# Maxima in a bank of the scores, block sums two at a time, and new instruction lists for one attention-and-FFN kernel

## The chip, the cores and the metric

The kernel runs on one core of a Trainium2 chip, as one program. The metric is the device time of one execution in microseconds, and runs of a kernel are compared by it.

## What is computed

Memory attention for 8 batches of 8 heads, 576 positions and head width 64, with 32 memories a head, and a bilinear feed-forward block behind it, in fp32.

```python
a = np.exp(phi - np.max(phi, axis=2, keepdims=True))
a = a / (np.sum(a, axis=2, keepdims=True) + 1e-09)
k_m = np.einsum('bhsm,bhsd->bhmd', a, k)
v_m = np.einsum('bhsm,bhsd->bhmd', a, v)
scores = scale * np.matmul(q, k_m.transpose(0, 1, 3, 2))
attn = softmax(scores)              # with 1e-09 added to the sum
x = np.matmul(attn, v_m)            # 4608 tokens x 512
out = ((x @ w1) * (x @ w2) @ w3) @ w_out
```

## The kernel before

One batch is 576 tokens, cut into two halves of 288 columns (`HALF`). The weights are prepared in a first phase: 64-bit words are converted to fp32 in five steps a task (C1 to C5), and w3 and w_out are multiplied once (W..., line 611), since no nonlinearity stands between them. After that each batch b does two things at once. Its attention step for batch b+1 or b+2 runs: maxima of phi over the positions (`top`), their exponentials and sums (`exp`, `norm`), the maxima spread over partitions by two transposes (`bm`, line 232, into a PSUM bank of its own), subtracted from a second copy of phi (`bs`, L238 and L242), exponentials (`be`), memories (`mem`, L254 and L263, scaled by `memc`), two transposes of them (`block`, L285, copied out by `blockc` on ScalarE), scores (`sc0`, `sc1`, L303), and the softmax (`scc` transposes into SBUF, `mx`, `sb`, `ex`, `sm`, `mu`, `tr`). M0 to M3 (L420) multiply the value memories with w1 and w2. Meanwhile the products of batch b run: block products P1 to P7 for four quarters q (`block_product`, L748, six matmuls a step and a Strassen-like scheme of seven products for four blocks), then the output units O1 to O7 in two parts (`out_unit`, L833, twelve matmuls a step). All of them are fp32 split into a high and a low part, three matmuls for one.

Between the P and the O steps stand sums of blocks: `first_sum` (tokens f, L789) and `sums` (Sa, Sb, Sc, L800 to L804), each for one block of four, on VectorE or GpSimd. `block_result` (tokens e, L773) adds a kept result in SBUF to one in PSUM, and `block_g` (tokens v, L732) multiplies two results; `a_copy` (tokens c) copies one of the factors.

The order of every engine's instructions is written out by hand in four lists of tokens: FIRST for batch 0 with the weights' phase, SECOND for batch 1, BATCH for batches 2 to 6, LAST for batch 7. Each engine takes its instructions in the order in which the lists name them. A token with a digit names the step, quarter or part; "!" moves a step that can run on two engines to the other one (f, Sa, Sb, Sc run on GpSimd without it and on VectorE with it; l, v and others the reverse). Attention tokens are for batch b+1, with "+" for b+2 and with "-" for b. Loads (`phi2`, `tok2`, `kv2`, `q2`) are issued by SyncE, whose queue also holds the stores of the results (C11 to C22).

PSUM has eight banks, four slots on each of two sides. `Pair` takes the first free slot of each side, and `done` returns them. The order of returns in the list decides which slot the next step takes, and that step waits for the last reader of the slot.

## Time and profile before

| | us |
|---|---|
| median of 3 runs | 497.23 (496.66 to 497.57) |
| the profiled execution | 496.72 |
| its span, from the first to the last instruction | 494.9 |
| TensorE busy | 489.1 |
| VectorE busy | 429.8 |
| ScalarE busy | 339.0 |
| GpSimd busy | 265.2 |

The span lies within the execution's time; the 1.8 us around it are start and end. Busy times are those of instructions, and overlapping instructions of one engine count once. In timelines a line gives the start and duration of one instruction or of several alike that follow each other; since matmuls overlap, the pace of TensorE is read from start to start. "Idle before" stands in square brackets with the engine that ended it.

### The profile page before, as it was taken

To read this page: it belongs to the slowest core of one execution; us is meant where nothing else is said; L and a number is where in the kernel's file an instruction comes from. 1 tells how busy PE (TensorE), PEld (TensorE's weight loads), DVE (VectorE), ACT (ScalarE), POOL (GpSimd) and SP (SyncE) were. 2 spreads that over 40 slices of the span, in tenths; PEclk is the share of its full clock that TensorE was granted. 3 is DMA by queue.
4 is the path that set the end of the run, shared out by engine and by line. 5 is a ranking of instruction groups with operands and counts; after the bars stand their busy time and mean duration, and the time that the engine had idled before them with its cause. 6 is when DMAs were issued, how large, how long until landed. Compare 5 with 4: busy or idle time off the path is not lost.

```text
span 494.9 us, 11317 instructions
## 1 busy us (share of the span) xinstructions
PE 489.1 (99%) x4328; PEld 422.2 (85%) x4328; DVE 429.8 (87%) x812; ACT 339.0 (68%) x718; POOL 265.2 (54%) x256
## 2 busy tenths in 40 slices
...
PEclk9999999999999999999999999999999999999999
...
GB/s 295 411 410 426 426 161 87 248 3 38 255 262 215 3 143 327 11 3 42 318 120 3 24 254 203 3 24 145 311 1 26 81 88 2 25 48 25 2 1 97
DMA packets 22390, 68.89 MB, mean 139 GB/s; under 512 B 1728, under 2 KB 9920, under 8 KB 20288
## 3 DMA queue, kind: packets, MB, share of 16 engines
...
q8 instruction: 34, 0.56, 0.5%
...
## 4 chain that ended last, share of the span: by engine, by line
PE 97%; DMA 1%; ACT 0%; DVE 0%; SPq 0%; issue 0%; DVEq 0%
PE ps L833 36%; PE ps L748 32%; PE ps L611 11%; PE ps L420 6%; PE ps L718 5%; PE ps L254 3%; PE ps L303 2%; DMA raw<-in_w3T 1%; PE ps L263 1%; PE ps L285 0%; PE ps L232 0%; SPq L527 0%; DVE wo L599 0%; ACT w L584 0%; DVE w L599 0%
## 5 line engine op out<-in xcount | busy, mean ns | idle before, releaser
L833 PE MATMUL ps<-sh,Wh 128*128 128x288 f32 x448 | 132.8, 296 | 0.0
L833 PE MATMUL ps<-sh,Wl 128*128 128x288 f32 x448 | 132.2, 295 | 0.0
L833 PE MATMUL ps<-sl,Wh 128*128 128x288 f32 x448 | 132.0, 295 | 0.0
L818 POOL TENSOR_TENSOR sl<-g,sh 128x576 fp32r<-128x576 f32 x43 | 65.3, 1520 | 72.8 <-ACT sh L501 48.9
L833 PEld LDWEIGHTS ps<-sh,Wh 128*128 128x128 f32 x448 | 84.2, 188 | 6.8 <-ACT mh L431 5.0
L833 PEld LDWEIGHTS ps<-sh,Wl 128*128 128x128 f32 x448 | 84.2, 188 | 0.0
L833 PEld LDWEIGHTS ps<-sl,Wh 128*128 128x128 f32 x448 | 84.2, 188 | 0.0
L501 ACT CAST sh<-g 128x576 fp32r<-128x576 f32 x78 | 52.3, 685 | 24.3 <-PE ps L833 14.5
L611 PE MATMUL ps<-wo,w 128*128 128x512 f32 x128 | 55.9, 594 | 0.2 <-DVE w L599 0.2
L767 ACT COPY c<-ps 128x288 f32<-128x288 f32 x112 | 41.6, 411 | 18.9 <-PE ps L748 16.2
L773 DVE TENSOR_TENSOR c<-ps,c 128x288 f32<-128x288 f32 x112 | 44.8, 451 | 10.4 <-ACT c L767 8.4
L748 PE MATMUL ps<-sh,ms 128*128 128x288 f32 x224 | 51.8, 296 | 0.0
L611 PEld LDWEIGHTS ps<-wo,w 128*128 128x128 f32 x128 | 24.0, 190 | 30.4 <-issue 28.3
L728 ACT COPY a_sb<-ps 128x288 f32<-128x288 f32 x72 | 29.0, 406 | 22.7 <-PE ps L748 19.8
L818 DVE TENSOR_TENSOR sl<-g,sh 128x576 fp32r<-128x576 f32 x55 | 43.2, 794 | 0.7 <-ACT sh L501 0.4
L438 DVE TENSOR_TENSOR ml<-ps,mh 128x512 fp32r<-128x512 f32 x64 | 41.0, 682 | 1.3 <-ACT mh L431 1.2
L748 PEld LDWEIGHTS ps<-sh,ms 128*128 128x128 f32 x224 | 38.2, 188 | 1.0 <-ACT ps L761 0.8
L732 DVE TENSOR_TENSOR g<-ps,a_sb 128x288 f32<-128x288 f32 x72 | 32.1, 449 | 6.2 <-ACT a_sb L728 5.0
L456 DVE TENSOR_TENSOR tmp<-ps,tmp 128x256 f32<-128x256 f32 x84 | 32.8, 418 | 4.4 <-ACT mh L431 2.1
L431 ACT CAST mh<-ps 128x512 fp32r<-128x512 f32 x64 | 34.5, 597 | 2.2 <-PE ps L420 1.2
L748 PE MATMUL ps<-ah,mh 128*128 128x288 f32 x112 | 34.6, 309 | 0.0
L748 PE MATMUL ps<-sh,mh 128*128 128x288 f32 x112 | 33.1, 296 | 0.0
...
## 6 DMA issues: line engine op xcount, KB each, us to landing
...
ph<-in_phiT SPq DMA_DIRECT2D x8, 576.0 KB, 4.6
a<-in_phi_tok SPq DMA_DIRECT2D x8, 576.0 KB, 5.7
...
```

Of the source, the lines that this page charges most:

```text
L420: nc.tensor.matmul(ps[t][g * M : (g + 1) * M], lhsT=vm[b % 2][d, g], rhs=w12_sb[q][d, :, g], start=True, stop=True,)
L431: nc.scalar.copy(out=mh[:, t], in_=ms["ps", q][t].rearrange("p (w f) -> p w f", w=2))
L438: nc.vector.tensor_tensor(out=ml[:, t], in0=x, in1=ms[q][0][:, t].bitcast(F32), op=ALU.subtract)
L456: nc.vector.tensor_tensor(out=tmp[:, j], in0=x, in1=tmp[:, y], op=op)
L501: nc.scalar.copy(out=out, in_=in_)
L611: nc.tensor.matmul(pw[r, i // 2][i % 2][:, cols], lhsT=x[:, i * P : (i + 1) * P], rhs=wos[k // half][:, k % half, cols], start=k == 0 and ...
L732: engine.tensor_tensor(out=G[n, f // half][:, f % half], in0=b, in1=a, op=ALU.mult)
L748: nc.tensor.matmul(G[bank, q][w][:, :HALF], lhsT=xs[x][:, w], rhs=ys[y], start=i in (1, 5) and k == 0, stop=i in (2, 3, 4) and k == 2, ski ...
L767: nc.scalar.copy(out=G["kept", i, q][:, j], in_=x)
L773: nc.vector.tensor_tensor(out=c, in0=x, in1=c, op=ALU.add)
L818: flexible().tensor_tensor(out=lo, in0=src, in1=hi.bitcast(F32), op=ALU.subtract)
L833: nc.tensor.matmul(ps[j][:, :HALF], lhsT=piece(x, s, 2 * part + k)[:, jc], rhs=y[:, k], start=i in first and part == 0 and k == 0 and t == ...
```

## The change

- `scores(1)` of batches 2 to 6 calls `spread_max` of the next batch with its own pair of banks: the two transposes go to columns 288 to 415 of the two banks, ahead of the score matmuls. `Pair` counts its users, and both banks are returned when the scores are copied out and the maxima are subtracted. `sub_max` then does its wide addition in two parts, one for each bank. Batches 0 to 2 keep the bank of their own.
- M3 of batches 2 to 6 is followed at once by `block` of the next batch.
- `first_sum` and `sums` take two blocks (`pair_of`) in one instruction.
- `block_result` for product 2 writes its second half back to PSUM, and `block_g` reads it there, always on VectorE; the bank is returned after that.
- The additions of 1e-9 move from VectorE to ScalarE; the reciprocal of `soft_sum` becomes a step of its own, `si`.
- `block_product` looks up the sums of the M blocks only where it uses them.
- All four lists are new.

```diff
 FIRST = """
...
-C4 C3 tok0 kv0 q0 C2 C3 C2 C5 C4 C5 -top -exp W06 -norm C1 C1 C2 C3 C2 C3 W07 -bm C4 C5 K2 Kh2 C4 C5 W101 C1 K3 Kt3
-W100 K1 W111 -bs K0 C4 Kt0 Kl2 C3 Kh1 Kh0 W110 C2 r3 C4 -be -mem C5 C3 Kt2 r0 C1 -memc -block C5 -blockc -sc0 -sc1
--scc0 -scc1 Kt1 W121 W120 -mx0 C3 C2 -sb0 W130 -mx1 -ex0 C2 Kl0 -sb1 C3 W131 W141 C4 -sm0 W140 -ex1 C1 C5 C1 W150 W160
...
-Sc0! O20 Mu0 M1 h21 l21 Sc2 h61 M2 l61 ex0 O21 sm0 O61 ex1 sm1 Sb1! Sb2! h70 l70! h71 mu1 Mr1 mu0 h50 l71 l50! u2 Ms1
...
+W01 W02 C5 C3 C2 C4 C5 W03 W04 W05 -top C1 -exp C1 C2 C3 W06 W07 C4 K1 K2 Kt2 Kt1 C5 C2 K0 K3 -bm Kh1! C4 C3 W100 C1
+-bs W101 C3 W110 Kh0! W111 -be Kh3 C4 C5 -mem C5 Kt3 Kh2 C2 C4 C3 W120 -norm -memc -block -blockc Kl3 C1 C5 -sc0 -sc1
+W130 Kl1 -scc0 -scc1 C3 C2 -mx0 W121 -sb0 -ex0 -mx1 C4 Kl0 -sb1 C2 C3 r1! -ex1 Kl2 Kt0 C1 C5 W131 W141 W140 r0! r3! C1
...
+l11 sb0 A30 a30 l41 sb1 O40 Sa0! Sa1! y0 Sb1 ex0 O11 g30 ex1 O41 Mr0 Ms0 h60 l60 p1 h20 O60 M1 Mt0 l20! sm0 O20 h21
+sm1 Sb0! Mu0 h61 l61 O61 h70 l70 h71 u2 l21 p4 si0 O21 h50 Sc1! q2 Sc0! O70 si1 Mr1 C11 h30 l71 mu1 h51 O71 mu0 Ms1
+Mt1 h31 Mh1 l50! M2 tr0 ah0 tr1 Mu1 l30 Mh2 l51! O50 O51 ah1 al1! p5 O30 l31 al0 T1 T3! Ml1 C21 C22 T2! T4! O31 C12
...
 """
 BATCH = """
-phi2 P10 -M3 s00 s01 P20 c10 v10 P60 k200 k201 P50 P70 k502 P30 e402 v40! e202 -Mr3 -Ms3 v20! P11 P40 s10 s11 c30 v30
-h10! -Mh3 P61 k210 k211 P51 +top -Ml3 -Mt3! P21 k512 P31 c11 e212 +exp -Mu3! P71 +bm P12 e412 P41 f0 v11 s20 s21 c31
-P62 sc1 tok2 +bs l10! v31 sc0 v41 kv2 scc0 scc1 k220 h11! P22 P52 v21! c12 v12 mx2 P13 k522 k221 P32 e222 f3 P72 s30
-+be P53 s31 P23 k532 P63 c13 e422 v42 k230 k231 v22 f1 l11! sb2 P33 e232 f2 P73 e432 v13 P42 Sa0 ex2 Sa1! P43 +mem v43
-c32 v32 Sb0 h20 +norm sm2 +memc M0 Mr0 M2 Sa3 c33 v33 v23! M1 O10 Mh0 Ms0 Ml0 Sb3 O11 Sb1 h21 l21 h50 Sa2! l20! p1 l50
-Sb2! h60 l60 O20 O21 Mh1 Sc1! h61 O60 C11 l61 O61 h51 h70 Mt0 Sc0! mu2 Mh2 u2 tr2 ah0 ah1 Sc2! l51! O50 Sc3! l70 h30
-h71 l71! O51 p5 Mu0 O70 al0 l30 O30 Ml1 h40 l40 T1 h31 l31 Mr1 Ms1 O71 O31 h41! C22 O40 C12 +block q2 l41! Mt1 +blockc
-T3! O41 Mu1 al1 T2 Th1 C21 Tl1 T4! Th0! Mr2 Tl0! Ms2 Mt2! Mu2! Ml2
+P10 s00 s01 -M3 P60 blockc P20 c10 v10 k200 k201 P50 phi2 P70 k502 e402 v40! P30 e202 v20 P11 P40 s10 s11 P61 +top
+-Mr3 c30 v30 k210 k211 -Ms3 -Mt3! P51 k512 P71 e412 -Mh3 h10! -Ml3 P21 P31 e212 v21 P41 P12 +exp f0 c11 v11 sc1 sc0
+c31 v31 v41! s20 s21 l10! scc0 P62 k220 k221 P52 h11 scc1 P72 P22 tok2 +bs k522 e422 f1 P32 -Mu3! c12 l11! v12 P13 s30
+e222 v22 s31 P42 c32 v42! +be P23 mx2 P63 k230 sb2 k231 P53 k532 ex2 kv2 c13 P73 e432 v32 P33 +norm e232 v23 Sa0 P43
+c33 +mem v33 M0 +memc Sb0 v13 Mh0 M2 Mr0 sm2 M1 Mh1 v43! O10 Ms0 Mt0 h21 h20! Ml0 Mu0 si2 O11 p1 l21 h50 Mr1 h60 l20!
+O20 O21 C11 l50 Sc0 Sa1 Sb1! l60 mu2 O50 h51 l51 h61 l61 h70 O60 O61 Mh2 Ms1 tr2 h71 Ml1 u2 h30 l70! O51 h40 l30 l71!
+l40 O70 p5 Sc1! ah0 Mt1 h41 q2 Ml2 O30 O71 al0! C22 O40 l41! O41 Mu1 T1 T3 h31 l31 ah1 al1 T2 T4! O31 Mr2 C12 C21 Ms2
+Th1 Tl1! Th0 Tl0! Mt2! Mu2!
 """
...
@@ -145,7 +144,7 @@
 
 
         def __init__(self, n=2, full=True, seeded=False):
-            self.slots, self.banks = [], []
+            self.slots, self.banks, self.users = [], [], 1
             for side in range(n):
                 slot = next(i for i in free_banks[side] if not seeded or (side, i) in written)
                 free_banks[side].remove(slot)
@@ -160,7 +159,9 @@
             return [(i, self.banks[i][:, :HALF]) for i in range(w.start, w.stop)]
 
         def done(self, *sides):
-            for i in sides or range(len(self.banks)):
+            if not sides:
+                self.users -= 1
+            for i in sides or range(len(self.banks) if self.users == 0 else 0):
                 free_banks[i].append(self.slots[i])
 
     loaded = {}
@@ -202,7 +203,7 @@
             LOADS[what](b)
 
 
-    ready = {}
+    ready, maxima = {}, {}
 
     def attention(b):
 
@@ -220,27 +221,37 @@
                 nc.scalar.activation(
                     out=ph[:, t], in_=ph[:, t], func=AF.Exp, bias=mx[:, t : t + 1], accum_out=sm[:, t : t + 1]
                 )
+            nc.scalar.activation(out=sm, in_=sm, func=AF.Copy, bias=1e-9)
 
         def norm():
-            nc.vector.tensor_scalar_add(v["sm"], v["sm"], 1e-9)
             nc.vector.reciprocal(out=v["sm"], in_=v["sm"])
 
-        def spread_max():
-            v["mxb"] = Pair(1, full=False)
-            ps = v["mxb"][0][:, : NT * P]
+        def spread_max(beside=None):
+            v["bank"] = beside or Pair(1, full=False)
+            if beside:
+                beside.users += 1
+                v["mxb"] = [beside[t][:, HALF : HALF + P] for t in range(NT)]
+            else:
+                v["mxb"] = [v["bank"][0][:, t * P : (t + 1) * P] for t in range(NT)]
             for t in range(NT):
-                nc.tensor.transpose(ps[:, t * P : (t + 1) * P], v["mx"][:, t : t + 1].broadcast_to([P, P]), ident)
+                nc.tensor.transpose(v["mxb"][t], v["mx"][:, t : t + 1].broadcast_to([P, P]), ident)
 
         def sub_max():
-            ps, n = v["mxb"][0][:, : NT * P], NT * P
+            n = NT * P
             v["a"] = loaded.pop(("a", b))
             a = v["a"][:, : 4 * n].rearrange("p (c x) -> p c x", c=4)
-            nc.vector.tensor_tensor(out=a, in0=a, in1=ps.unsqueeze(1).broadcast_to([P, 4, n]), op=ALU.add)
+            if len(v["bank"].banks) == 1:
+                ps = v["bank"][0][:, :n].unsqueeze(1).broadcast_to([P, 4, n])
+                nc.vector.tensor_tensor(out=a, in0=a, in1=ps, op=ALU.add)
             for t in range(NT):
+                if len(v["bank"].banks) == 2:
+                    x = a[:, :, t * P : (t + 1) * P]
+                    ps = v["mxb"][t].unsqueeze(1).broadcast_to([P, 4, P])
+                    nc.vector.tensor_tensor(out=x, in0=x, in1=ps, op=ALU.add)
                 half = slice(t * D, (t + 1) * D)
                 x = v["a"][half, 4 * n :]
-                nc.vector.tensor_tensor(out=x, in0=x, in1=ps[half, t * P : (t + 1) * P], op=ALU.add)
-            v["mxb"].done()
+                nc.vector.tensor_tensor(out=x, in0=x, in1=v["mxb"][t][half], op=ALU.add)
+            v["bank"].done()
 
         def exp_tok():
             nc.scalar.activation(out=v["a"], in_=v["a"], func=AF.Exp)
@@ -297,6 +308,8 @@
             if "q" not in v:
                 v["q"] = loaded.pop(("q", b))
             banks = v["scores", n] = Pair()
+            if n == 1 and 2 <= b < B - 1:
+                maxima[b + 1](banks)
             ps = [banks[t][:, :HALF] for t in range(NT)]
             for g in range(NG):
                 for t in range(NT):
@@ -316,7 +329,7 @@
             for t in range(NT):
                 x = ps[t][:, :HALF].rearrange("p (k m) -> p k m", m=M)
                 nc.vector.transpose(out=v["s"][:, n, t * nb : (t + 1) * nb], in_=x)
-                ps.done(t)
+            ps.done()
 
         def both(n):
             return slice(0, 2) if n == 2 else slice(n, n + 1)
@@ -342,8 +355,10 @@
         def soft_sum(n):
             ss = v["ss", n] = stats(n)
             nc.vector.tensor_reduce(out=ss, in_=v["s"][:, both(n)], axis=AX.X, op=ALU.add)
-            nc.vector.tensor_scalar_add(ss, ss, 1e-9)
-            nc.vector.reciprocal(out=ss, in_=ss)
+            nc.scalar.activation(out=ss, in_=ss, func=AF.Copy, bias=1e-9)
+
+        def soft_inverse(n):
+            nc.vector.reciprocal(out=v["ss", n], in_=v["ss", n])
 
         def soft_mul(n):
             sv, ss = v["s"][:, both(n)], v["ss", n]
@@ -395,9 +410,10 @@
             flexible().tensor_tensor(out=lo, in0=src, in1=hi.bitcast(F32), op=ALU.subtract)
             ready["T", b][n].append(lo)
 
+        maxima[b] = spread_max
         steps = {"top": top, "exp": exp, "norm": norm, "bs": sub_max, "be": exp_tok, "memc": normal, "blockc": spread,
                  "bm": spread_max, "mem": memories, "block": blocks}
-        parts = {"sc": scores, "scc": tokens_down, "mx": soft_max, "sb": soft_sub, "ex": soft_exp, "sm": soft_sum,
+        parts = {"sc": scores, "scc": tokens_down, "mx": soft_max, "sb": soft_sub, "ex": soft_exp, "sm": soft_sum, "si": soft_inverse,
                  "mu": soft_mul, "tr": probs, "ah": probs_high, "al": probs_low, "Th": sums_high, "Tl": sums_low}
         for name, f in parts.items():
             steps |= {f"{name}{n}": lambda f=f, n=n: f(n) for n in range(3)}
@@ -732,9 +748,9 @@
         engine.tensor_tensor(out=G[n, f // half][:, f % half], in0=b, in1=a, op=ALU.mult)
 
     def block_product(b, i, q, G):
-        (mh, ml), (sh, sl) = ready["M", b][q], ready["M", b]["sums", q]
+        of = ready["M", b]
         t, u = {1: (0, 0), 2: (1, 0), 4: (1, 1), 7: (0, 1), 5: (None, 0), 6: (None, 1), 3: (None, 2)}[i]
-        xs = [m[:, t, :, u * P : (u + 1) * P] for m in (mh, ml)] if t is not None else [m[:, u] for m in (sh, sl)]
+        xs = [m[:, t, :, u * P : (u + 1) * P] for m in of[q]] if t is not None else [m[:, u] for m in of["sums", q]]
         if i < 4:
             ys = ready["A", b][{1: (0, 0), 2: (0, 1), 3: (1, 1)}[i]]
         else:
@@ -770,8 +786,8 @@
         bank, kept = {2: ("gamma", 2), 4: ("alpha", 5)}[i]
         for j, x in G[bank, q].parts(w):
             c = G["kept", kept, q][:, j]
-            nc.vector.tensor_tensor(out=c, in0=x, in1=c, op=ALU.add)
-            if i == 2:
+            nc.vector.tensor_tensor(out=x if (i, j) == (2, 1) else c, in0=x, in1=c, op=ALU.add)
+            if (i, j) == (2, 0):
                 G[bank, q].done(j)
 
     def block_g(i, q, G, engine):
@@ -782,15 +798,23 @@
             bank.done(1)
         else:
             c = G["kept", {2: 2, 4: 5}[i], q]
-            g_product(G, n, f, c[:, 0], c[:, 1], engine)
-
-    def first_sum(k, G):
+            if i == 2:
+                g_product(G, n, f, c[:, 0], G["gamma", q][1][:, :HALF], nc.vector)
+                G["gamma", q].done(1)
+            else:
+                g_product(G, n, f, c[:, 0], c[:, 1], engine)
+
+    def pair_of(part):
+        return slice(2 * part, 2 * part + 2)
+
+    def first_sum(part, G):
+        k = pair_of(part)
         low, top = G[1, 0][:, k], G[0, 0][:, k]
         flexible().tensor_tensor(out=low, in0=top, in1=low, op=ALU.subtract)
 
-    def sums(which, k, G):
-
-        gp = flexible().tensor_tensor
+    def sums(which, part, G):
+
+        gp, k = flexible().tensor_tensor, pair_of(part)
         a, s3, a22, a12 = G[0, 0][:, k], G[1, 0][:, k], G[1, 1][:, k], G[0, 1][:, k]
         if "S2" not in G:
             G["S2"] = att.tile([P, NG, S], F32, name="q", tag="q").rearrange("p g s -> p (g s)")[:, : half * HALF]
@@ -906,6 +930,8 @@
                 if name in steps[0]:
                     if at < B:
                         steps[at][name]()
+                    if what == "-M3" and 2 <= b < B - 1:
+                        steps[b + 1]["block"]()
                 elif what in at_stage:
                     next(at_stage[what])()
                     left -= what == "C5"
```

## Rows read from the trace of the kernel before

**Rows 1.** The page, parts 1 and 2: TensorE's busy time, granted clock by slice.

```profile
PE 489.1 (99%) x4328; PEld 422.2 (85%) x4328; DVE 429.8 (87%) x812; ACT 339.0 (68%) x718; POOL 265.2 (54%) x256
...
PEclk9999999999999999999999999999999999999999
```

**Rows 2.** Windows: us; busy PE, PEld, DVE, ACT, POOL; steady, last batch.

```profile
344.86:397.42 52.56, 52.56 (x524) 48.40 (x516) 47.30 (x92) 35.03 (x82) 31.79 (x31) 1.00 0.32 121
452.95:494.90 41.95, 38.67 (x296) 38.23 (x288) 25.88 (x51) 20.54 (x48) 16.86 (x15) 0.99 0.09 29
```

**Rows 3.** TensorE's timeline, steady batch: start us, duration us, engine, line, tiles.

```profile
344.86 0.40 PE L748 MATMUL ps<-ah,mh 128*128 128x288 f32 x1
...
354.50 0.38 PE L232 MATMUL ps<-ident,mx 128*128 128x128 f32 x2
354.64 0.38 PE L748 MATMUL ps<-ah,mh 128*128 128x288 f32 x1
...
358.40 0.40 PE L748 MATMUL ps<-ah,mh 128*128 128x288 f32 x1
```

**Rows 4.** TensorE's timeline, the same stretch one batch later.

```profile
397.42 0.40 PE L748 MATMUL ps<-ah,mh 128*128 128x288 f32 x1
...
410.65 0.40 PE L748 MATMUL ps<-ah,mh 128*128 128x288 f32 x1
```

**Rows 5.** TensorE's timeline, end of a batch and M3 of the next.

```profile
341.15 0.38 PE L285 MATMUL ps<-ident,kvm 128*128 128x128 f32 x2
341.29 0.38 PE L833 MATMUL ps<-sh,Wh 128*128 128x288 f32 x1
...
343.84 1.09 PE L420 MATMUL ps<-w,vm 64*32 64x512 f32 x16
```

**Rows 6.** TensorE's timeline, transposes between matmuls of the first phase.

```profile
37.06 0.38 PE L232 MATMUL ps<-ident,mx 128*128 128x128 f32 x2
37.28 1.02 PE L611 MATMUL ps<-wo,w 128*128 128x512 f32 x2
```

**Rows 7.** TensorE's timeline, first phase: block transposes, M0 and M1, first products.

```profile
47.10 0.59 PE L285 MATMUL ps<-ident,kvm 128*128 128x128 f32 x2 [0.53 <-ACT kvm L276]
...
67.00 1.95 PE L420 MATMUL ps<-w,vm 64*32 64x512 f32 x32
68.88 3.70 PE L611 MATMUL ps<-wo,w 128*128 128x512 f32 x8
...
72.69 0.29 PE L718 MATMUL ps<-ah,ml 128*128 128x288 f32 x1
```

**Rows 8.** VectorE's timeline, first phase: `Ml0`.

```profile
68.81 1.28 DVE L438 TENSOR_TENSOR ml<-ps,mh 128x512 fp32r<-128x512 f32 x2
```

**Rows 9.** VectorE's timeline, the steady batch of rows 3: Ms3, v30, `+top`.

```profile
349.52 1.20 DVE L456 TENSOR_TENSOR tmp<-ps,tmp 128x256 f32<-128x256 f32 x3
350.79 0.46 DVE L732 TENSOR_TENSOR g<-ps,a_sb 128x288 f32<-128x288 f32 x1
351.16 1.34 DVE L214 TENSOR_REDUCE mx<-ph 128x2 f32<-128x1152 f32 x1
```

**Rows 10.** SyncE's timeline there, and DMA issues: size, median us to landing.

```profile
344.17 0.46 SPq L170 DMA_DIRECT2D ph<-in_phiT  x1
...
ph<-in_phiT SPq DMA_DIRECT2D x8, 576.0 KB, 4.6
```

**Rows 11.** Groups by line and shape: count, busy us, mean ns, idle before.

```profile
L818 POOL TENSOR_TENSOR sl<-g,sh 128x576 fp32r<-128x576 f32 x43 | 65.3, 1520 | 72.8 <-ACT sh L501 48.9 <-issue 17.7 <-DVE g L804 5.1
...
L773 DVE TENSOR_TENSOR c<-ps,c 128x288 f32<-128x288 f32 x112 | 44.8, 451 | 10.4 <-ACT c L767 8.4 <-ACT a_sb L728 1.0 <-PE ps L748 0.9
L818 DVE TENSOR_TENSOR sl<-g,sh 128x576 fp32r<-128x576 f32 x55 | 43.2, 794 | 0.7 <-ACT sh L501 0.4
...
L345 DVE TENSOR_SCALAR st<-st 128x36 f32<-128x36 f32 x6 | 4.7, 778 | 0.2
...
L232 PE MATMUL ps<-ident,mx 128*128 128x128 f32 x16 | 3.1, 275 | 0.0
```

More of the change, by code (lines that the diff above doesn't have):

```diff
@@ new lines @@
+-tr0 C5 -M1 -tr1 s0 s1 C4 -ah0! -al0 C5 -Mh1 Q1! -ah1! C3 -Ml0 W171 Dt2 A01 -Ml1 Dt0 -al1! C4 Dt3 F3 a01 A00 C1 C2 g01
+C5 a00 F0 g00 A11 -M2 D2 E2 Et2 a11 D3 C1 g11 E3 -Mh2 Et3 Et0 phi1 -Ml2 C3 C1 Q2! A03 C4 C4 A10 a03 g03 A23 C5 C3 F2
+a23 g23 A12 a10 r2 w2! A02 D1 a12 g10 A13 top s2 C5 a02 g02 t0 exp y2 bm z0 a13 Dt1 F1 g12 tok1 bs A22 g13 h10 a22 A20
+Et1 w3 t2 be kv1 -M3 -Mh3 E1 a20 mem D0 f0 q1 -Ml3 norm A33 h11 memc block w1 Q0 blockc g22 f1 A32 y3 t3! g20 z3 E0
+h40 y1 a32 Q3 sc1 l10! w0 g32 a33 sc0 scc0 mx0 g33 t1 z1 M0 Mh0 Ml0 l40! A31 h41 a31 g31 A21 z2 a21 scc1 g21 O10 mx1
@@ L49 @@
-l51! O70 h41 Ml0 +block +blockc l50 Sc1! O71 O50 ah0 O51 al0 ah1 Ms0 l41 C11 al1! T1 h30 T3 h40 Sc3! l30 l40 M1 p5
-Sc2! C22 Mt0 h31! l31! T2! Mh1 q2 Mu0 M2 Mh2 Mr1 Ms1 O30 Mt1 T4! Th0! Ml1 O40 Mu1 Th1 O41 C21 O31 Tl1! Tl0! C12 Mr2
-Ms2 Mt2! Mu2! Ml2
+P10 s00 s01 P11 P20 c10 s10 v10 P60 k200 P50 k201 P70 k502 e402 P30 e202 s11 v20 phi1 top P61 k210 k211 tok1 P21 c11
+P51 k512 P71 bm e412 exp P40 P31 c30 v11 bs P41 c31 v30 be P12 v41 -M3 v31 h11! h10! -Mr3 e212 l11! kv1 -Mh3 v21 f1
+norm s20 phi2 mem s21 P62 k220 -Ms3 P22 memc block -Ml3 P52 -Mt3 +top tok2 c12 v12 k221 P72 k522 blockc e422 P32 sc1
@@ new lines @@
++exp e222 l10! v22 sc0 scc0 P13 s30 s31 v40 P42 P23 +bs c13 scc1 +be -Mu3! c32 P63 k230 k231 v13 f0 v42! Sa0 Sb0 v32
+O10 O11 p1 h20 P53 P73 mx2 k532 sb2 ex2 l20! +norm e432 v43! P33 e232 h71 h60! v23 P43 c33 sm2 v33 O20 kv2 +mem M0 si2
+Sa1! h21 h61 l21 O21 h70 l71! mu2 C11 Mr0 l60 O60 +memc Sb1! Sc1! l61 O61 u2 Ms0 Mt0 Mh0 Sc0! h50 tr2 l70! h51! l51
+O70 O71 M1 Mu0 M2 l50! Ml0 h30 ah0 ah1! Mh1 q2 l30 O50 h40! Mr1 Ml1 h31 Ms1 O51 l31 p5 C22 O30 O31 l40 al0! T1! h41
+Mt1 Mu1 l41 Mr2 T3! al1 Mh2 T2 C12 T4 Th0! Th1 Tl1! Ml2 O40 O41 C21 Tl0! Ms2 Mt2! Mu2!
@@ L62 @@
+Th1 Tl1! Th0 Tl0! Mt2! Mu2!
 """
 LAST = """
-Mr1 P10 s00 s01 P11 +bm P20 P60 k200 Ml1 k201 P50 P70 c10 v10 k502 e402 P30 e202 Mr0 T1 +be P40 c30 v20! -M3 v40 s10
-s11 P61 v30 h10 -Mh3 -Ml3 phi2 f0 sb2 l10! ah0 P51 k210 kv2 k211 P71 k512 e412 -Mr3 M2 Mu0! -Ms3 -Mt3 P31 e212 P21 tr2
-sc1 Mt0 P12 s20 s21 scc1 Ms2 Mh0 v41! v21 P41 c31 v31 Mt2! +block f3! al1 q2 P22 c12 v12 P52 k522 +blockc c11 -Mu3!
-P62 k220 k221 T2 P32 Mr2 e222 v11 P53 P72 f1! v22 k532 P13 e422 f2! v42 Sa0 Sa1 P33 +top h11 s30 s31 P63 k230 k231 Mh2
```

33 lines of the change are left out of this document (12 added, 21 removed).

## The prediction, made before the changed kernel was run

> **What bounds the kernel now.** I began with the engines' busy times and the granted clock on the page [rows 1]: TensorE is busy for 489.1 of 494.9 us and its clock stands at the upper level, 2.4 GHz, in every slice. So nothing is to be had from the clock, and 5.8 us of the span at most from TensorE's idle time. Then I read the busy times of one batch in the steady middle [rows 2]: in 52.56 us TensorE is busy 52.56 us, VectorE 47.30, ScalarE 35.03, GpSimd 31.79. The other engines are lighter than TensorE by 5 us and more in every batch. Work taken from them or moved between them shortens nothing as long as TensorE never waits. What can shorten the kernel is TensorE's own sequence: fewer changes between kinds of matmul, and the few waits that are left.
>
> The changes have a price, and the timeline of TensorE shows it. I read it by starts, since durations overlap. The stream of 128x288 products advances by about 0.131 us each (72 of them fill 9.64 us between 344.86 and 354.50, 0.2 of it at the ends) [rows 3]. In the steady batch the two transposes that spread the maxima (L232) stand alone between products. From the re-entry after M3 at 344.86 to the products behind the scores at 358.40 it takes 13.54 us [rows 3]. One batch later there is no batch left to prepare, the same 90 products and the same 32 score matmuls run without these transposes, and the stretch takes 410.65 - 397.42 = 13.23 us [rows 4]. So a lone visit of two transposes costs 0.31 us, of which 0.14 are the transposes (354.50 to 354.64) and the rest is leaving and re-entering the stream. The two transposes of the block step (L285) stand alone in the same way, 341.15 to 341.29 [rows 5].
>
> **The change, part by part.**
>
> *Transposes that no longer stand alone.* The maxima's transposes of batches 3 to 7 go into the bank of `sc1`, directly ahead of its matmuls, and the block transposes of batches 3 to 7 go directly behind M3. Walking the lists and keeping only TensorE's steps, ten lone visits vanish: five of L232, five of L285. Each frees 0.31 us and puts the two transposes next to small matmuls. What they cost there no row shows. The nearest rows are 0.14 us for the pair alone [rows 3, 5] and 0.22 us for a pair between fp32 matmuls (37.06 to 37.28) [rows 6]; the far end is 0.31, nothing gained. I take 0.19, nearer the second, because there too the neighbours are fp32. Gain 0.12 each, 1.2 us for ten; range 0 to 1.7.
>
> A rule of the Trainium skill speaks against this. The rows: one transpose lasts 275 ns [rows 11], yet two follow each other so closely that the pair takes 0.14 us from start to start [rows 3]. The Trainium skill, "TensorE: Matmul & The Clock Gate", section "Part 4: PE-mode transpose", gives about 275 ns for a transpose in a kernel's context and puts most of it down to access latency; if that latency did not overlap, a pair would take 0.55 us. The trace agrees with the duration but shows the overlap; it doesn't show it beside row-tiled matmuls, so this is a rival below.
>
> *Order in the first list.* M1 and M2 of batch 1 ran as one cluster and are now apart. Two M steps in one cluster take 1.88 us (67.00 to 68.88) [rows 7]; one alone takes 1.02 (343.84 to 344.86) [rows 3, 5], so two take 2.04, and the extra re-entry of the stream is 2.55 - 18 x 0.131 = 0.19 (341.29 to 343.84) [rows 5]. Loss 0.35 us. In exchange W120 is moved between the memories of batch 0 and their block transposes, where TensorE idled 0.53 us for `kvm` of ScalarE [rows 7]. W120 is four matmuls of L611, well over a microsecond, so it covers the wait; another entry and exit eats some 0.2 of it (an estimate, from the 0.19 above). Gain 0.3; range 0 to 0.5. What is late next: the scores of batch 0 come about 1 us later, and VectorE's softmax after them, while the first products come 0.5 us earlier. `Ml0` ended at 70.1 [rows 8], TensorE wanted it at 72.69 [rows 7]. I added up VectorE's work between the scores and `Ml0` in both lists and it is equal within 0.3 us, so some 0.8 us of cover remain.
>
> *Work of the other engines.* Block sums in pairs: eight instructions of 576 a batch for sixteen of 288. On VectorE 0.79 against 2 x 0.45 us (price of L818 for the wide one), 0.1 us saved a pair; on GpSimd the wide one lasts 1.52 us [rows 11], and I take the same 0.1 there. The small addition behind the row sums leaves VectorE (0.78 us for 36 columns [rows 11]) and becomes two short ScalarE instructions; the reciprocal now waits for ScalarE, and soft_mul behind it, but a step of its own (`si`) places it several instructions later. sub_max's wide addition splits into two, which costs under 0.1 us of VectorE. Counting every step of the repeated list with these prices, VectorE goes from 47.3 to some 44.2 us a batch, GpSimd from 31.8 to 34.4, ScalarE from 35.0 to 36.5. All stay under 52.5: cost or gain nothing, with TensorE's products as cover. Without that cover VectorE's 3 us would be the gain.
>
> *The sum left in PSUM.* VectorE writes the second half of result 2 over its PSUM input instead of `c`, and the product v2 reads it there. No row has VectorE writing PSUM; its reads from PSUM and its writes to SBUF are in the 0.45 us [rows 11], so I take 0 and leave -0.1 to +0.1 us for each, four a batch on VectorE, which has slack. It does hold one gamma bank longer, by one VectorE instruction.
>
> *New waits.* In the repeated list VectorE gets `+top` (1.34 us) ahead of v30 instead of behind it [rows 9]. P51 on TensorE needs the bank that v30 frees; behind P51 the whole stream queues. Before, v30 ran at 350.79 and P51's second half wanted it at about 344.86 + 8.5 x 0.79 = 351.6. Now `Ms3` goes behind v30 and `+top` takes its place: if phi has landed, `+top` can start near 349.9 and v30 end near 351.6, against a need at 351.8 (0.2 later for the block transposes). SP's queue has changed with it: the phi load waits behind C12's store, whose two additions (0.9 us) follow the last output unit O31. It was issued at 344.17 and took 4.6 us [rows 9, 10]; now some 0.75 later, landing near 349.5. I put this at 0, up to 0.35 a batch in the four batches that have it.
>
> *The last batch.* From 452.95 on TensorE works through 288 products and is busy 38.67 us [rows 2]; 288 x 0.131 + 0.2 is 37.9, so some 0.6 to 0.7 us are short waits for results of other engines. The new order can keep or lose them; I take 0.3 gained, range -0.5 to +0.6.
>
> Sum: -1.2 + 0.35 - 0.3 - 0.3 = -1.45 us. The profiled execution took 496.72 us, 1.8 more than its span, and the median of the runs is 497.23, 0.5 above it. Applied to the median: 495.8 us.
>
> **Rivals.** *Nothing left after all.* The transposes cost as much in a cluster as alone, or small waits of the new order return what was saved. For it: ten gains of 0.12 us are easily lost, since every step of every list has moved. Against: the other engines become lighter or stay far under TensorE. Time: -0.65 to +0.9 around 497.2, so 496.3 to 498.1, say 497.1.
>
> *The load of phi blocks VectorE (slower).* If phi lands later than about 350.2 in the clock of that batch, 1.4 us after its former landing, VectorE stands at `+top`, v30 behind it, P51 and all products behind that. Every 0.5 us beyond this costs 2 us over the four batches. For it: the issue moved behind a store that waits for VectorE itself, and my estimate uses up half of the cover. Against: 0.7 us are left. One microsecond late gives 495.8 + 4 = 499.8; half of one gives 497.8.
>
> *Transposes at full latency inside a cluster (slower).* A pair costs 2 x 0.275 = 0.55 us [rows 11] against 0.31 for the lone visit: 10 x 0.24 = 2.4 us lost in place of 1.2 gained, 499.4 us. Against: the overlap in [rows 3, 6], both without row tiling. This is what the page named above would give.
>
> *The change does not do what it says:* if the transposes still came apart from the score matmuls, the gain would shrink to that of the block step; this is inside the second case.
>
> **How the numbers follow.** Forecast 495.8, chance 0.57, own range 494.3 to 496.6; no change 0.27; phi 0.13; latency 0.03. What a measurement of this kernel can tell from no change is about 0.2%, 1.0 us: faster is below 496.24, slower above 498.2. Of the forecast's chance 0.05 falls within that bound, of the second case 0.04 falls below it and of the phi case 0.03 stays within. So faster 0.56, same 0.31, slower 0.13. The range for 8 in 10 runs from 494.3 (497.23 - 1.7 + 0.35 - 0.5 - 0.6 = 494.8 with every term at its good end, less 0.5 for the spread of the runs shown) to 498.5, which takes in the second case and the milder half of phi.
>
> **What would show it.** In the new timeline of TensorE: L232 directly ahead of L303 and L285 directly behind L420 in batches 2 to 6, the batch some 0.24 us shorter than 52.57, a pair at 0.14 to 0.22 us; L285 of batch 0 without idle time before it. Wrong would be: TensorE waits behind v30 or `+top` (a hole at P51), a batch as long as before, idle time ahead of the first product of L718, or holes in the last batch above 0.6 us. The forecast falls if a batch is not shorter though nothing waits: then the cost of changing kinds is misread.

## The result, and the profile after

The changed kernel takes 499.7 us (median of 6 runs, 498.89 to 500.14), the kernel before 496.87 in the runs beside it: a ratio of 1.0055, with a 95% interval of 1.0045 to 1.0065. It is 2.8 us slower, where 1.4 us faster was forecast. The profiled execution took 500.04 us, near the slowest of the six; its span is 498.3. The page's busy times and granted clock:

```profile
PE 491.2 (99%) x4328; PEld 421.8 (85%) x4328; DVE 412.7 (83%) x757; ACT 345.9 (69%) x738; POOL 268.1 (54%) x232
PEclk9999999999999999999999999999999999999999
```

Against [rows 1] TensorE has the same 4328 instructions at the same clock, VectorE is 17 us lighter, and the span is 3.4 us longer. One steady batch in the table of windows (two before the one of [rows 2]; columns as there):

```profile
240.05:292.82 52.77, 52.77 (x519) 48.44 (x517) 44.18 (x84) 36.95 (x86) 32.60 (x27) 1.00 0.32 113
```

TensorE still counts as busy throughout, yet the batch takes 52.77 us instead of 52.57. Busy time can't show where they went: a matmul that is issued and stands for its operands or bank can count as busy (M0 below does). So I took TensorE's starts. Its order is fixed by the lists, so every start can be given to its step, and the time from one step's first start to the next step's is what the step cost. Summed by list, in us, from the timelines of several profiled executions (the other kernels are the experiments below; batch 3 is the second run of the repeated list, and the last column is TensorE's whole stretch):

| kernel | first phase | second batch | batch 3 | batch 5 | batch 6 | last | all |
|---|---|---|---|---|---|---|---|
| before | 120.06 | 55.71 | 52.57 | 52.57 | 49.95 | 46.15 | 482.13 |
| after | 121.13 | 56.66 | 52.77 | 53.08 | 50.39 | 45.86 | 485.46 |
| q3 | 120.65 | 56.08 | 52.77 | 52.81 | 50.68 | 45.86 | 484.42 |
| q3b | 119.96 | 55.93 | 52.77 | 52.83 | 50.68 | 45.87 | 484.30 |
| phi | 121.14 | 56.09 | 52.71 | 52.70 | 50.39 | 45.87 | 484.30 |
| mend3 | 119.87 | 55.45 | 52.61 | 52.92 | 50.59 | 45.86 | 482.52 |
| best2 | 119.85 | 55.47 | 52.57 | 52.57 | 49.96 | 45.87 | 481.59 |

So the 3.3 us come from the first phase (1.07), the second batch (0.95), the repeated list (0.2 in three batches, 0.5 and 0.4 in two) and go back by 0.3 in the last. Three places account for most of the loss; a fourth is where the gain was forecast.

**M0 of batch 1 in the first phase** (the expectation of q3 counts from one and calls it batch 2). TensorE's timeline (start, us, line, tiles, how many):

```profile
97.91 1.20 PE L316 MATMUL ps<-q,km 64*32 64x288 f32 x32
98.91 2.23 PE L436 MATMUL ps<-w,vm 64*32 64x512 f32 x16
101.08 0.40 PE L734 MATMUL ps<-ah,mh 128*128 128x288 f32 x1
```

A lone M step takes 1.02 us [rows 3, 5]; this one takes 2.17. Its weight loads name what they waited for, and VectorE's timeline shows what stood ahead of that:

```profile
100.06 0.18 PEld L436 LDWEIGHTS ps<-w,vm 64*32 64x32 f32 x14 [1.04 <-DVE g L748]
```

```profile
97.17 2.34 DVE L970 TENSOR_TENSOR w<-w 64x1024 f32<-64x1024 f32 x1
99.55 0.46 DVE L748 TENSOR_TENSOR g<-ps,a_sb 128x288 f32<-128x288 f32 x1
```

The bank comes from g32 (99.55), and g32 stands behind Q3, the 2.34 us subtraction on the last weights.

**The memories of the second batch.**

```profile
142.81 1.09 PE L436 MATMUL ps<-w,vm 64*32 64x512 f32 x16
145.04 0.43 PE L265 MATMUL ps<-kv,a 128*32 128x128 f32 x8 [1.14 <-ACT mh L447]
```

1.14 us between M3 and the first product of the memories. The view names ScalarE's `mh`, which ended at 144.906; the second of the two large loads of `kv`, which the first product reads, landed at 144.91. Two candidates at the same instant: see kvorder.

**P51, where `+top` now stands ahead of v30** (VectorE, then TensorE):

```profile
194.50 1.34 DVE L215 TENSOR_REDUCE mx<-ph 128x2 f32<-128x1152 f32 x1
195.76 0.45 DVE L748 TENSOR_TENSOR g<-ps,a_sb 128x288 f32<-128x288 f32 x1
```

```profile
196.07 0.59 PE L764 MATMUL ps<-sh,ms 128*128 128x288 f32 x2
196.50 0.30 PE L764 MATMUL ps<-sl,ms 128*128 128x288 f32 x1
```

The bank is free at 196.21, when v30 ends, and the product behind it starts 0.43 us after the first of the pair, where 0.26 is the pace. P51 takes 0.18 us too long. In batch 6, which has no `+top`, it takes 0.10 too long.

**The merged transposes.**

```profile
188.15 1.09 PE L436 MATMUL ps<-w,vm 64*32 64x512 f32 x16
189.16 0.44 PE L296 MATMUL ps<-ident,kvm 128*128 128x128 f32 x2
189.36 0.38 PE L764 MATMUL ps<-sh,ms 128*128 128x288 f32 x1
...
200.74 0.38 PE L237 MATMUL ps<-ident,mx 128*128 128x128 f32 x2
201.05 1.20 PE L316 MATMUL ps<-q,km 64*32 64x288 f32 x32
```

They stand where the lists put them, ahead of L316 and behind L436. From start to start the maxima's pair takes 0.31 us and the blocks' pair 0.20; alone both took 0.14 [rows 3, 5].

### The profile page after: what moved, and what is told of

It is laid out like the page before. It is cut to its first block, busy times and chain, and to the rows that moved or that the text cites. A ratio compares the mean times of both kernels' runs of the same rounds, so it can differ in the third digit from the quotient of the medians.

```text
span 498.3 us, 11202 instructions
## 1 busy us (share of the span) xinstructions
PE 491.2 (99%) x4328; PEld 421.8 (85%) x4328; DVE 412.7 (83%) x757; ACT 345.9 (69%) x738; POOL 268.1 (54%) x232
## 4 chain that ended last, share of the span: by engine, by line
PE 95%; DVE 2%; DMA 1%; issue 1%; ACT 0%; SPq 0%; POOL 0%; DVEq 0%
PE ps L857 36%; PE ps L764 31%; PE ps L627 11%; PE ps L436 6%; PE ps L734 5%; PE ps L265 3%; PE ps L316 2%; DMA raw<-in_w3T 1%; PE ps L274 1%; DVE g L748 1%; DVE w L970 0%; PE ps L296 0%; PE ps L237 0%; DVE ml L454 0%; ACT mh L447 0%
## 5 line engine op out<-in xcount | busy, mean ns | idle before, releaser
L517 ACT CAST sh<-g 128x576 fp32r<-128x576 f32 x80 | 54.2, 680 | 14.7 <-PE ps L857 10.6
L764 PE MATMUL ps<-sh,ms 128*128 128x288 f32 x224 | 53.2, 304 | 0.0
L748 DVE TENSOR_TENSOR g<-ps,a_sb 128x288 f32<-128x288 f32 x72 | 31.4, 450 | 19.6 <-ACT a_sb L744 19.2
L842 DVE TENSOR_TENSOR sl<-g,sh 128x576 fp32r<-128x576 f32 x53 | 40.5, 769 | 6.8 <-ACT sh L517 5.1
L789 DVE TENSOR_TENSOR c<-ps,c 128x288 f32<-128x288 f32 x84 | 35.4, 452 | 8.4 <-ACT c L783 6.4
L447 ACT CAST mh<-ps 128x512 fp32r<-128x512 f32 x64 | 34.4, 592 | 5.9 <-PE ps L436 5.9
L777 ACT COPY ps<-ps 128x288 f32<-128x288 f32 x56 | 21.0, 385 | 20.4 <-PE ps L764 13.7
L436 PE MATMUL ps<-w,vm 64*32 64x512 f32 x512 | 33.2, 595 | 0.1
```

The source lines that it names most:

```text
L436: nc.tensor.matmul(ps[t][g * M : (g + 1) * M], lhsT=vm[b % 2][d, g], rhs=w12_sb[q][d, :, g], start=True, stop=True,)
L447: nc.scalar.copy(out=mh[:, t], in_=ms["ps", q][t].rearrange("p (w f) -> p w f", w=2))
L517: nc.scalar.copy(out=out, in_=in_)
L748: engine.tensor_tensor(out=G[n, f // half][:, f % half], in0=b, in1=a, op=ALU.mult)
L764: nc.tensor.matmul(G[bank, q][w][:, :HALF], lhsT=xs[x][:, w], rhs=ys[y], start=i in (1, 5) and k == 0, stop=i in (2, 3, 4) and k == 2, ski ...
L789: nc.vector.tensor_tensor(out=x if (i, j) == (2, 1) else c, in0=x, in1=c, op=ALU.add)
```

## Experiments

All are edits of the changed kernel, timed beside the kernel before; "us" is the median.

**1. Q3 out of VectorE's way: q3, q3b.**

```diff
- a32 Q3 sc1 ... z2 a21
+ a32 sc1 ... z2 Q3! a21          (q3: on GpSimd, four steps later)
+ P30 e202 s11 Q3! v20            (q3b: on GpSimd, second list)
```

> The subtraction on the last weights (L970, 2.34 us on VectorE at 97.17) is taken from in front of g32 and given to GpSimd four steps later, where GpSimd idles. Theory: M0 of batch 2's memory (98.91 to 101.08, 2.17 us where a lone M takes 1.02) stands for 1.15 us because its PSUM bank is freed by g32, and g32 stands behind that subtraction in VectorE's order. Then M0 takes about 1.02 us and all that follows comes 1.1 us earlier: 498.6 us. Rival: VectorE is busy for 3.9 of every 4 us there, so what M0 gains is waited for a few steps later on: 499.5 to 499.9.

Measured: 498.65, ratio 1.0044 (1.0031 to 1.0056). The time is the theory's, the way to it isn't: the first phase got only 0.48 us shorter. M0 takes 1.02 us again, but a hole stands ahead of O60:

```profile
111.14 0.29 PE L857 MATMUL ps<-sh,Wl 128*128 128x288 f32 x1
111.95 0.41 PE L857 MATMUL ps<-sl,Wh 128*128 128x288 f32 x1 [0.52 <-DVE sl L842]
```

`sl` is late because VectorE was held up beside GpSimd, which had the next step right behind Q3 (VectorE, GpSimd):

```profile
105.22 1.84 DVE L349 TENSOR_TENSOR s_sb<-s_sb,st 128x576 f32<-128x576 f32 x1
106.99 0.75 DVE L842 TENSOR_TENSOR sl<-g,sh 128x576 fp32r<-128x576 f32 x1
```

```profile
102.28 2.40 POOL L970 TENSOR_TENSOR w<-w 64x1024 f32<-64x1024 f32 x1
104.76 1.69 POOL L651 TENSOR_TENSOR Wl<-sl,Wh 128x512 fp32r<-128x512 f32 x1
```

L349 lasts 0.75 us elsewhere. The rest of the gain lies in the second batch, where TensorE stood 0.6 us for the load of the memories in place of 1.1 (see kvorder), and that differs between executions.

> The subtraction on the last weights is taken out of VectorE's order in the first phase and given to GpSimd at the start of the second batch, where GpSimd idles from 136.4 to 143.3 in the trace. In the kernel with it four steps later on GpSimd the wait of M0 went (1.17 us), but VectorE's L349 lasted 1.84 us beside it where it lasts 0.75 alone, and a new hole of 0.8 us stood ahead of O60. Theory: that hole was GpSimd's doing; now none is left in the first phase, and it is 1.1 us shorter: 498.6 less the 0.6 us that the load's wait gave back there, 498.0. Rival: VectorE has no room there whoever takes the subtraction, the hole comes back elsewhere: 498.6 as before.

Measured: 497.86, ratio 1.0025 (1.0015 to 1.0035). The first phase is 1.17 us shorter, M0's whole wait, and no hole came back.

**2. What the memories waited for: kvorder, mend2, mend3.**

```diff
- for t in range(NT):
-     for i in (2, 3, 0, 1):
+ for i in range(4):
+     for t in range(NT):
```

> The products of the memories take the tokens' chunks in the order in which their two loads are issued (0, 1, 2, 3) in place of (2, 3, 0, 1). Theory: in the second batch the first product of L265 waits for the second of the two loads, which lands at 144.91, and starts at 145.04, 1.14 us after M3; the first load landed at 142.45, so with the new order it starts right behind M3, half of the products run under the rest of the wait, and about 0.2 us of it is left: 498.8 us. Rival: it waits for ScalarE's mh copy, which ends at 144.906 and which the table of waits names: no change, 499.7.

Measured: 499.56, ratio 1.0051 (1.0037 to 1.0064): no gain that can be told. The theory's first half holds, since the memories now start right behind M3, so it was the load and not `mh`. But 0.5 us later they stand again:

```profile
144.04 0.43 PE L265 MATMUL ps<-kv,a 128*32 128x128 f32 x8
144.76 0.54 PE L265 MATMUL ps<-kv,a 128*32 128x128 f32 x12 [0.30 <-DVE g L748]
```

The new order asks for the second bank after 8 products instead of 32, and that bank is freed by v21 on VectorE. To part the two, mend2 loads phi of the third batch at the end of the first phase, ahead of the rush (it also has q3b, kvorder, phi and the swap of mend, below); mend3 is mend2 with the old order of chunks.

```diff
- v20 phi1 top                       tr0 ah0 tr1 Mu1
+ v20 top                            tr0 ah0 tr1 phi2 Mu1
```

> As the run called mend, with phi of the third batch loaded at the end of the first phase instead of at the start of the second batch, where the DMA engines are busy from 134.6 on. Theory: of the 0.5 us for which the memories still wait for their second load in that run, nothing is left, because 0.58 MB ahead of that load are gone: 497.3. Rival: the load waits at its new place for its buffer and holds SP's queue, or the stretch has another bound behind it: 497.8.

> As the run called mend2, with the memories' chunks in their old order (2, 3, 0, 1). Theory: with phi of the third batch loaded early the two loads of the memories land by 142.3 and hold nothing any more; the 0.5 us that were left in mend2 are a wait for v21's bank, which the other order of the chunks asks for 0.6 us sooner. Then the second batch takes 55.45 us of TensorE in place of 55.95: 497.3. Rival: the bank is waited for in either order: 497.9.

Measured: mend2 497.91, ratio 1.0023 (1.0013 to 1.0034); mend3 497.24, ratio 1.0007 (0.9998 to 1.0016). In mend2 the load landed at 141.4, before it was asked for, and the 0.5 us stayed; in mend3 they are gone and the second batch takes 55.45 us. So the load was the wait of the changed kernel, and the reordering had put a bank in its place. How long the load holds TensorE differs between executions: the hole was 1.1 us in the profile of after, 0.7 in that of apart, 0.4 to 0.6 in those of q3, q3b, top and phi, none in that of onesum.

**3. `+top` and VectorE's slack: top, three, phi.**

```diff
- P61 +top -Mr3 c30 v30 k210
+ P61 -Mr3 c30 v30 +top k210                                   (top)
+ -M3 P60 blockc +top P20 ... tr2 ... u2 phi3 h30, no phi2     (phi)
```

> In the repeated list the maxima of the next batch (1.34 us of VectorE) go behind c30 and v30 in place of ahead of them. Theory: they hold v30 and with it the bank of P51; the holes at P51 (0.18 us in three batches, 0.27 and 0.20 ahead of it in the fourth) go: -0.5 us or more, 499.1. Rival: batch 6 has a hole of 0.10 there with no such maxima, so only the difference of 0.07 a batch goes: 499.4.

Measured: 503.23, ratio 1.0128 (1.0114 to 1.0142). Both theories fail: 3.5 us slower, 0.93 in each of four batches. The hole at P51 shrank to the 0.11 of batch 6, and TensorE stood further on: 0.3 us in the products ahead of the transposes and 0.6 inside them:

```profile
200.26 0.27 PE L237 MATMUL ps<-ident,mx 128*128 128x128 f32 x1
200.99 0.32 PE L237 MATMUL ps<-ident,mx 128*128 128x128 f32 x1 [0.46 <-DVE g L748]
```

They need the second bank of `sc1`. VectorE frees it with v21 (L748), which reads there the sum left in PSUM by L789; v21 ends at 200.93, the second transpose starts at 200.99. It stands at the end of VectorE's queue, and v30 at its head had waited:

```profile
199.99 0.46 DVE L789 TENSOR_TENSOR ps<-ps,c 128x288 f32<-128x288 f32 x1
200.48 0.46 DVE L748 TENSOR_TENSOR g<-ps,c 128x288 f32<-128x288 f32 x1
```

```profile
194.94 0.46 DVE L748 TENSOR_TENSOR g<-ps,a_sb 128x288 f32<-128x288 f32 x1 [1.10 <-ACT a_sb L744]
```

In the changed kernel `+top` fills these 1.1 us. From there to the transposes VectorE has no slack at all, though it is busy for only 44.2 of 52.8 us in the batch.

> The three edits together. If the three waits are what the new lists lost, the gains add: 499.7 - 1.1 - 0.9 - 0.5 = 497.2, about the kernel before. If they cover each other (the load is issued earlier when the first phase is shorter, and lands earlier by as much), less than the sum: 498.0 or more.

Measured: 503.32, ratio 1.0129 (1.0115 to 1.0143), as top alone (503.23): beside its loss the two other edits gained nothing that can be told.

> In the repeated list phi is loaded in the batch before, behind the last use of its buffer, and the maxima (1.34 us of VectorE) go to the batch's start, where VectorE idles for 2.25 us. Theory: from P51 to the maxima's transposes VectorE has no slack (moving the maxima behind v30 cost 0.93 us a batch there); taking 1.34 us out of that stretch ends the holes at P51 (0.18 us in three batches, 0.47 in the fourth) and the wait inside the transposes: 498.7. Rival: the holes come from ScalarE's copies and TensorE's own order: 499.6; and if phi's early load delays the load of q behind it, slower.

Measured: 498.61, ratio 1.0033 (1.0021 to 1.0045). `+top` now runs where VectorE idled, and v30 no longer follows it:

```profile
187.85 1.34 DVE L215 TENSOR_REDUCE mx<-ph 128x2 f32<-128x1152 f32 x1
...
194.78 0.46 DVE L748 TENSOR_TENSOR g<-ps,a_sb 128x288 f32<-128x288 f32 x1 [1.10 <-ACT a_sb L744]
```

The time is the theory's; of the mechanism only part. P51 keeps 0.11 us, so 0.07 a batch went; batch 5 gave 0.4, most of it an extra that only some executions have. The other half of the gain in this profile lies in the second batch, whose load came earlier in this execution, and is not the edit's. What the edit takes away is a risk, since phi is there long before `+top`; the profile of q3b happened to catch it (VectorE, TensorE):

```profile
299.65 1.35 DVE L215 TENSOR_REDUCE mx<-ph 128x2 f32<-128x1152 f32 x1 [0.62 <-DMA ph<-in_phiT]
```

```profile
301.42 0.41 PE L764 MATMUL ps<-sh,ms 128*128 128x288 f32 x1 [0.61 <-DVE g L748]
```

There phi landed 0.6 us late in one batch, `+top`, v30 and P51 followed, and the batch took 53.49 us, 0.7 more than its neighbours. The runs of phi lie within 0.21 us, those of the changed kernel within 1.25; that this risk makes the difference is not shown.

**4. The price of a visit: apart.**

```diff
- banks = Pair(); if n == 1: maxima[b + 1](banks)
+ sc1 sc0 ... P62 +bm k220      (same bank, after the scores and one block product)
```

> The maxima's transposes of batches 3 to 7 stay in the bank of sc1, but stand one block product behind the scores, alone between products. By the price in the prediction (0.31 us alone, 0.19 merged) five visits cost 0.6 us: 500.3. By the starts in the trace of the changed kernel (0.31 us merged, of which 0.08 is the change to the scores' small tiles that the stream pays anyway and 0.04 a wait for the bank; 0.22 alone) it makes no difference: 499.6 to 499.8.

Part of the block products' sums comes out changed in this kernel, so it serves for its times alone; TensorE's instructions are the same in number and shape. Measured: 499.73, ratio 1.0057 (1.0044 to 1.007), as the second reading has it. The window of batch 4 is 52.78 us as in the changed kernel (in this execution batch 3 was 0.35 us longer, by a wait in the output units):

```profile
292.56:345.34 52.78, 52.78 (x519) 48.49 (x517) 44.13 (x84) 36.94 (x86) 32.69 (x27) 1.00 0.32 113
```

Merged or alone in that bank, a pair of transposes costs the same.

**5. New work or new order: oldorder, hybrid, oldorder2, hybrid2, onesum.** The first four put the new work (sums over two blocks at the place of the later one, the addition on ScalarE; no merged transposes, the sum in `c`) into the old lists, the hybrids with first phase and last batch of the new ones; onesum puts the old sums and `c` into the new lists. oldorder (518.61) and hybrid (513.79) had all four products of result 2 on VectorE by an oversight, and tell only that VectorE has no room for them.

> As the run called oldorder, with the products of result 2 on the engine that the old lists name: there all four of a batch had come to VectorE by an oversight, and one of them lasted 1.63 us beside GpSimd, where it lasts 0.46 alone, and TensorE stood 1.33 us at P72 in every batch. Theory: the new work by itself costs and gains nothing: 496.5 to 497.2. Rival: the sums that now wait for the later of two blocks hold up the output units in the first two batches (3.7 us at O11, 2.3 at O71 in that run): 500 to 507.

> As the run called hybrid, with those products on the old engines. If the new work is free in the old order, the stretches add to 496.3. If the second batch keeps the waits at O11 and O60 of that run (3.7 and 1.5 us), 501 to 502, with the repeated batches back at 52.6.

> The changed kernel in its own order, with block sums taken one block at a time again and the sum of result 2 written to c. Theory: in its own order the new work is what VectorE's cover allows: sums one by one cost VectorE and GpSimd under 1 us a batch, hidden, and only the product of result 2, which then has both inputs in SBUF, may be held up beside GpSimd: 499.7 to 501. Rival: VectorE has no room from P51 to the maxima's transposes, so a product of 1.6 us there comes out in full: 0.5 to 1.2 us a batch, 502.5 to 506.

Measured: oldorder2 510.08, ratio 1.0265 (1.025 to 1.0279); hybrid2 506.38, ratio 1.0196 (1.0182 to 1.021). Both lie beyond the worst case that I had expected. The steady batch takes 52.57 us in both, as before: there the new work is free and worth nothing. Elsewhere it isn't: in oldorder2 the second batch takes 61.39, 5.7 more, the first phase 4.1 and batch 6 2.7 more; in hybrid2 the second batch takes 63.35. From oldorder2's table of waits (total, times, longest):

```profile
PE ps L851 <- DVE sl L836: 3.8, 3, 2.0
PE ps L851 <- ACT ps L869: 3.5, 1, 3.5
```

L851 is the output units. The longest wait, 3.5 us in the second batch of both kernels, is not one for a sum of two blocks. O60 waits for `p1`, ScalarE's copy out of its bank (L869). Ahead of that in ScalarE's queue stands the small addition (L356), and it waits for VectorE's row sums (VectorE, ScalarE):

```profile
166.44 1.34 DVE L355 TENSOR_REDUCE st<-s_sb 128x36 f32<-128x1152 f32 x1
```

```profile
167.81 0.23 ACT L356 ACTIVATE st<-st 128x36 f32<-128x36 f32 x1 [4.35 <-DVE st L355]
167.95 0.66 ACT L515 CAST sh<-g 128x576 fp32r<-128x576 f32 x1
168.51 0.69 ACT L869 COPY ps<-ps 128x288 f32<-128x288 f32 x2
```

In the kernel before the addition is VectorE's own, and there `p1` starts at 160.05, ahead of the row sums at 161.12. In the first phase and in batch 6 the waits are for `sl`, on VectorE, whose instructions were stretched beside GpSimd: two of L363 took 3.88 us in the first phase, where they take 1.42 in the kernel before. Behind the long waits TensorE's clock was also lower; the window behind O60's (columns as in [rows 2]):

```profile
168.96:172.40 3.44, 3.44 (x14) 3.44 (x15) 1.12 (x3) 2.29 (x4) 0.30 (x1) 0.52 0.02 5
```

The granted clock is 0.52, the lower level of 1.2 GHz, and the products start 0.24 us apart where 0.13 is the pace; behind the wait of 2.0 us in the first phase it was the same. That is some 1.6 us more each time, 3.2 of the 9.7 us that the first phase and the second batch lost. How much of the rest the pairs themselves cost is not separated.

Measured for onesum: 499.7, ratio 1.0063 (1.005 to 1.0076). Its steady batch is 52.97, 0.2 longer than with the pairs, while the load's wait was absent in its profile. So in the new order the pairs and the sum in PSUM together give 0.2 us a batch. In the old order it is above all the small addition that stands in the way, by the trace; no run parts it from the rest.

**6. The repairs together: mend.** q3b, kvorder and phi, with `O30 O71` exchanged, so that C22's copy is done before O40 writes its bank again (a start-to-start of 0.23 us at 235.19 where 0.13 is the pace).

> The subtraction moved as in q3b, the memories' chunks in the order of their loads, phi's load and maxima moved as in the run of that name, and O71 ahead of O30 in the repeated list, so that C22's copy has 1.6 us before O40 writes its bank again (0.09 us of waiting in each of five batches). If the terms add: 499.7 - 1.2 - 0.6 - 0.5 - 1.0 - 0.45 = 496.0, a little under the kernel before. If VectorE is the bound in the second batch too, 497 to 498.

Measured: 497.82, ratio 1.0019 (1.001 to 1.0028), 1.8 above the sum. The exchange gave its 0.1 a batch. Not gained: the 0.5 us of v21's bank that kvorder brought in; 0.3 in batch 5, where P61 still waits; 0.3 in batch 6, where the scores now wait for a bank; and P51's last 0.1 a batch.

**7. What is worth keeping: best, best2.** First, second and last list new, with q3b and the early phi; the repeated list old, sums one by one.

> First phase, second batch and last batch in the new order with the two repairs (the subtraction taken out of the first phase, phi of the third batch loaded early); the repeated list in the old order, without merged transposes from the fourth batch on, block sums one block at a time, the sum of result 2 in c, the small addition on ScalarE. By the stretches measured: 119.96 + 55.45 + 4 x 52.6 + 49.95 + 45.86 = 481.6 us of TensorE against 482.1 in the kernel before: 496.2. If the borders between the lists cost waits, 497 to 498.

Measured: 499.43, ratio 1.005 (1.0037 to 1.0062). The borders cost 3 us. One piece is a mishap of mine (ScalarE's copies ahead of the seeds), the other tells something. VectorE and GpSimd, with the sum in `c`:

```profile
135.45 2.32 DVE L748 TENSOR_TENSOR g<-c 128x288 f32<-128x288 f32 x1
```

```profile
135.06 2.40 POOL L971 TENSOR_TENSOR w<-w 64x1024 f32<-64x1024 f32 x1
```

> As the run called best, with two things mended that its trace showed. There the product of result 2 had both inputs in SBUF and lasted 2.32 us on VectorE (135.45 to 137.78) beside the subtraction on GpSimd (135.06 to 137.46), the maxima behind it came late, and TensorE stood 1.25 us; here the sum is left in PSUM in the first two batches and the last. And ScalarE's copies of the third batch's blocks come behind the seeds s00 and s01 (they stood ahead of them, 1.7 us). Theory: both holes go, and by the stretches 481.6 us of TensorE are left: 496.3 to 496.6. Rival: the product's length is not what held the maxima, and 497.5 or more is left.

Measured: 496.43, ratio 0.999 (0.9981 to 0.9999), faster than both kernels, by 0.5 us over the one before, just clear of the noise. The second batch gave 1.30 us, the third, where the copies are, 1.68. The same two instructions, with the sum left in PSUM:

```profile
135.76 0.46 DVE L748 TENSOR_TENSOR g<-ps,c 128x288 f32<-128x288 f32 x1
```

```profile
135.38 2.40 POOL L976 TENSOR_TENSOR w<-w 64x1024 f32<-64x1024 f32 x1
```

## Why the prediction was wrong, step by step

**Transposes that no longer stand alone (forecast -1.2): wrong, and the step is the price of a visit.** I took 0.31 us from two stretches, with and without the transposes [rows 3, 4], as if they differed by nothing else. They do. The scores themselves (before, with and without):

```profile
357.19 1.28 PE L303 MATMUL ps<-q,km 64*32 64x288 f32 x32
```

```profile
409.52 1.20 PE L303 MATMUL ps<-q,km 64*32 64x288 f32 x32
```

To the next product it is 1.21 us in one and 1.13 in the other, because `sc0` waited 0.08 for a bank. It was free when VectorE's subtraction of the maxima (L242) ended, at 357.21:

```profile
356.64 0.58 DVE L242 TENSOR_TENSOR a<-a,ps 64x128 f32<-64x128 f32 x2
```

So a visit alone cost 0.22, 0.14 and 0.08 for the re-entry, and the rest of the 0.31 was a wait behind the maxima. Merged I took 0.19; measured are 0.31 less the 0.09 that the stream pays ahead of the scores in any case, so 0.22: merging the maxima's pair gained nothing, as apart confirms. What went is the wait: in the changed kernel the scores take 1.13 in every batch of the repeated list. The blocks' pair went from 0.22 to 0.17 (0.19 + 0.08 for the re-entry behind it, less the 0.10 of the re-entry behind M3 alone). That is 0.14 a batch in place of 0.24, some 0.7 us of the 1.2, and most of it for another reason than the one I gave. The rival of full latency (0.55 a pair) didn't come either.

**The first list (+0.35, -0.3): the signs right, both miscounted.** Two M clusters came apart, not one (M0 and M1 of batch 0 too); together they lost 0.32 besides M0's wait. Memories and blocks of batch 0, with W120 between, won 0.8, of which the W products' new entries took 0.3 back.

**Other engines' work (0): the load was right, the conclusion not.** VectorE came to the 44.2 us that I had counted (GpSimd to 32.6, not 34.4), and TensorE stayed the longest engine. But the cover isn't spread evenly: from `+top` to the transposes VectorE has none (top), and in the first phase Q3 ahead of g32 stood TensorE for 1.15 us (q3b). I compared sums per batch where each wait is decided by what stands ahead of one instruction in a queue. This step is the main failure: the two waits in the first two lists, 1.17 and 1.1 us of the 3.3 that the profiled execution lost, have no term in the sum; q3b and mend3 took them away. For a change that rewrites all lists, each bank and each load that TensorE asks for needed a look at what stands ahead of its release.

**The sum left in PSUM (0): right in the price of the write, blind to its use and to the bank.** VectorE's write to PSUM lasts 0.46 us. What it buys shows in best and best2. What it costs is the bank, which I had named and not priced: it is held until v21 ends, 0.48 us after the write in top, and it is this bank that the transposes in top and the memories in kvorder waited for.

**`+top` ahead of v30 (0, up to 0.35): the right place.** Measured 0.18 a batch, 0.07 of it `+top`'s own. The phi rival exists as described, but in the profiles it came in the repeated list once, in q3b. In the profile of the changed kernel phi landed ahead of every `+top` (at 192.34 for the one at 194.50), so that its 499.7 us lie beside that rival's 499.8 is chance.

**The last batch (-0.3): right**, 46.15 to 45.86, but the 0.3 was a choice within -0.5 to +0.6 and not a reading.

**The second case's range.** -0.65 to +0.9 around 497.2 is 496.6 to 498.1, not 496.3 to 498.1; no chance hangs on it.

Also unforeseen were 0.09 us at O40 and 0.05 at O20 in each batch; why O20 waits I have not tried. Batch 5's extra 0.3 us, and 0.3 more at the scores of batch 6 (50.68 in place of 50.39 in the table), came in some kernels and not in others; why stays open.
